# Two DMAs instead of eight for 128 rows of w4, and two instead of four for wo, in a decode kernel that is bound by its loads

## Chip, cores and metric

One core of one Trainium2 chip. The metric is the device time of one execution in microseconds (us). A kernel is run several times. The time given is the median of its runs. Smaller is better. "2%" is the size from which a change counts as faster or slower.

## The reference

One decode step for B = 4 sequences, D = 576, in bfloat16: sliding-window attention and an MLP side by side, summed. Cut to what matters:

```python
W = 2048                                  # window: the last 2048 of 8192 cached positions
q = (xn @ wq)                             # 32 heads of 128
k, v = k_cache[:, :, -W:], v_cache[:, :, -W:]      # 16 kv heads, 2 q heads share one
p = softmax(q @ k.T * 128 ** -0.5)
attn = (p @ v) @ wo                       # wo: 4096 x 576
mlp = gelu(layernorm(...) @ w3) @ w4      # w3: 576 x 4608, w4: 4608 x 576
out = x + attn + xn + mlp                 # the mixer between is zero for one position
```

All is done once per sequence, so each weight and each cached key and value is read once: 87.17 MB from HBM.

## The kernel before

It loads K and V one kv head at a time (2.1 MB, six buffers), in the order K0 K1 K2 V0 K3 V1 K4 ..., and the weights between them. All large loads are issued by SyncE (`nc.sync`) on one queue, and this queue serves the 16 DMA engines of the core. The last loads are six pieces of w4. Each output is the sum of many small matmuls that accumulate into `acc`.

`w4` has 4608 rows, 36 x 128. 35 blocks of 128 rows are loaded in pieces over all 16 engines. The last 128 rows, the "apart rows", are loaded by themselves, because which engines carry a DMA depends on its shape (in this trace such a DMA ends with 5, 3 or 1 semaphore packets instead of 16). With them the author fills up engines that would otherwise end early.

```python
# 100 rows over five engines ("A"), 12 over three ("C"), 16 on engine 0 alone (six pieces, "B")
def x4_rows(part):
    if part == "A":
        src = B_w4[X0 + 28:F, :].rearrange("(q g i) n -> g q (i n)", q=4, g=5)
        nc.sync.dma_start(out=t[0:NX, XA * D:XS * D], in_=src)
    elif part == "C":
        src = B_w4[X0 + 16:X0 + 28, :].rearrange("(q g) n -> g q n", q=4)
        nc.sync.dma_start(out=t[0:12, XC * D:XA * D], in_=src)
    else:
        q, lo, hi = part                  # two or four rows into one partition
        ...
X_AFTER = {13: ["A", (0, 0, 4)], 14: [(1, 0, 4), (2, 0, 2), "C"], 15: [(2, 2, 4), (3, 0, 2), (3, 2, 4)]}
...
wo_src = A_wo.rearrange("(s p i) n -> s p (i n)", p=P, i=WOR)    # four groups of 1024 rows
def load_wo(p):                                                  # before V0, V4, V8 and V12; two buffers
    t = wop.tile([P, WOR, D], BF16, tag="wo", name="wo_sb")
    nc.sync.dma_start(out=t[:].rearrange("p i n -> p (i n)"), in_=wo_src[p])
...
mlp_extra(XC, XS)         # 12 matmuls on the apart rows, ahead of the last V
...                       # last V, projection's preparation
mlp_extra(XB, XC)         # 8 matmuls of 4 rows
o_proj(hl)                # last projection with wo
for lo, hi in pieces:     # w4, 35 blocks x 2 matmuls
    mlp_out(lo, hi)
# then two casts of acc into fin, and the output DMA
```

By rows, the sixteen engines carry 40, 24, 24, 20, 20 apart rows on engines 0 to 4 and none on 5 to 15.

Of the kernel before, what the change touches and what calls it, by code (L numbers as in the profile page):

```python
# [11 lines left out]
BF16 = mybir.dt.bfloat16  # L12
# [10 lines left out]
def kernel(  # L23
# [14 lines left out]
    nc = tc.nc  # L38
    P = 128
    B, Sq, D = A_x.shape  # L40
# [4 lines left out]
    F = B_w3.shape[1]  # L45
# [30 lines left out]
    pad.tile([P, PAD], F32, name="pad")  # L76
    kvp = ctx.enter_context(tc.tile_pool(name="kv", bufs=NKV))
    wp = ctx.enter_context(tc.tile_pool(name="w", bufs=1))
    wop = ctx.enter_context(tc.tile_pool(name="wo", bufs=2))
    ktp = ctx.enter_context(tc.tile_pool(name="kt", bufs=2))  # L80
    ptp = ctx.enter_context(tc.tile_pool(name="pt", bufs=2))
    bigp = ctx.enter_context(tc.tile_pool(name="big", bufs=2))
# [8 lines left out]
    w_tiles = {}  # L91
    wo_tiles = {}
    kv_tiles = {}
    WOH = 8
    WOR = WOH
    WOD = P // WOH
    WOQ = WOH // rep
    wo_src = A_wo.rearrange("(s p i) n -> s p (i n)", p=P, i=WOR)

    def load_kv(kind, h):  # L100
        win = k_win if kind == "K" else v_win
        t = kvp.tile([P, NC, Dh], BF16, tag="kv", name=f"{kind.lower()}n")
        nc.sync.dma_start(out=t[:].rearrange("p c d -> p (c d)"),
                          in_=win[:, h].rearrange("b (p c) d -> p b (c d)", c=NC))
        kv_tiles[kind, h] = t

    first = wop.tile([P, WOR * D], BF16, tag="wo", name="first")
    cut = {"at": 0}

    def part(n, parts=P):  # L110
# [10 lines left out]
    nc.sync.dma_start(out=wq_sb[:, 0:KJ * NQ], in_=wq_main)  # L121

    def load_wo(p):
        t = wop.tile([P, WOR, D], BF16, tag="wo", name="wo_sb")
        nc.sync.dma_start(out=t[:].rearrange("p i n -> p (i n)"), in_=wo_src[p])
        wo_tiles[p] = t

    def load_w3():
        t = wp.tile([P, KJ * F + F // 2], BF16, tag="w", name="w3_sb")
        nc.sync.dma_start(out=t[:, 0:KJ * F], in_=B_w3[0:KJ * P, :].rearrange("(p j) f -> p (j f)", j=KJ))  # L130
        nc.sync.dma_start(out=t[:, KJ * F:], in_=B_w3[KJ * P:D, :].rearrange("r (e f) -> (r e) f", e=2))
        w_tiles["w3"] = t
# [1 line left out]
    NFM = NF - 1  # L134
    W4_PIECES = [0, NFH, NFM - 11, NFM - 6, NFM - 2, NFM - 1, NFM]
    X0 = F - P
    XB, XC, XA = 0, 4, 5
    XS = 10
    NX = 20
    NS = NFM + XS  # L140

    def x_cols(ap):
        b, c, a = ap[:, 0:16], ap[:, 16:28], ap[:, 28:P]
        return [(0, b.rearrange("p (q i) -> p i q", q=4)), (16, c.rearrange("p (q g) -> p g q", q=4)),
                (28, a.rearrange("p (q g i) -> p i g q", q=4, g=5))]

    def load_w4():
        t = wp.tile([P, NFM, D], BF16, tag="w", name="w4_sb")
        for lo, hi in zip(W4_PIECES, W4_PIECES[1:]):
            e = lo // NFH  # L150
            n = NFH - e
            src = B_w4[e * (F // 2):e * (F // 2) + P * n, :].rearrange("(p i) n -> p i n", i=n)
            nc.sync.dma_start(out=t[:, lo:hi, :], in_=src[:, lo - e * NFH:hi - e * NFH, :])
        w_tiles["w4"] = t

    def load_x4():
        t = kvp.tile([P, NC, Dh], BF16, tag="kv", name="x4")
        w_tiles["x4"] = t[:].rearrange("p c d -> p (c d)")

    def x4_rows(part):  # L160
        t = w_tiles["x4"]
        if part == "A":
            src = B_w4[X0 + 28:F, :].rearrange("(q g i) n -> g q (i n)", q=4, g=5)
            nc.sync.dma_start(out=t[0:NX, XA * D:XS * D], in_=src)
        elif part == "C":
            src = B_w4[X0 + 16:X0 + 28, :].rearrange("(q g) n -> g q n", q=4)
            nc.sync.dma_start(out=t[0:12, XC * D:XA * D], in_=src)
        else:
            q, lo, hi = part
            src = B_w4[X0 + 4 * q + lo:X0 + 4 * q + hi, :].rearrange("(q i) n -> q (i n)", q=1)  # L170
            nc.sync.dma_start(out=t[q:q + 1, (XB + lo) * D:(XB + hi) * D], in_=src)

    X_AFTER = {13: ["A", (0, 0, 4)], 14: [(1, 0, 4), (2, 0, 2), "C"], 15: [(2, 2, 4), (3, 0, 2), (3, 2, 4)]}


    ident_bf = const.tile([P, P], BF16)
# [22 lines left out]
    op = const.tile([P, WOR, B], BF16, name="op")  # L199
# [5 lines left out]
    def acc_of(i):  # L205
        return accs[i * 2 // NI][i * QD:i * QD + B, :]


    def acc_matmuls(terms):
        for lhsT, rhs in terms:  # L210
            for i in range(NI):
                nc.tensor.matmul(out=acc_of(i), lhsT=lhsT, rhs=rhs[:, i * CW:(i + 1) * CW],  # L212
                                 start=False, stop=False, skip_group_check=True)
# [44 lines left out]
    for kb in range(NQD):  # L258
        nc.gpsimd.tensor_copy(out=sel[:, :, :, kb, :],
                              in_=ident_bf[:].rearrange("p (ib i e) -> p ib e i", ib=2, e=2))  # L260
# [19 lines left out]
    with nc.allow_low_precision("zeros and ones"):  # L280
# [7 lines left out]
                          in_=sel_j[:].unsqueeze(1).to_broadcast([P, NG, NJ]))  # L288
# [38 lines left out]
    for r in range(2):  # L327
        nc.vector.tensor_copy(out=q_bf[:, r],
                              in_=qT_ps[:, r].rearrange("p u (g x) -> p g u x", g=NQD)[:, :, :, 0:B])
# [5 lines left out]
    for kb in range(NQD):  # L335
        rows = slice(kb * QD, (kb + 1) * QD)
        dst = qz[rows, ZP:].rearrange("p (x m) -> p x m", m=P)[:, :, kb * QD:kb * QD + NJ].rearrange("p x (b r) -> p x b r", r=rep)
        src = qs_ps[rows].rearrange("p h i r b -> p (h i) b r")
# [89 lines left out]
    def o_scale(h):  # L428
        O_sb[h] = bigp.tile([P, NSL, Dh], F32, tag="big", name="O_sb")
        nc.scalar.activation(out=O_sb[h][:], in_=O_ps.pop(h)[:], func=ACT.Copy, scale=st.pop(("rd", h)))  # L430
# [39 lines left out]
    def o_proj(h):  # L470
        if h % WOQ < WOQ - 1:
            return
        acc_matmuls([(op[:, i, :], wo_tiles[h // WOQ][:, i, :]) for i in range(WOR)])

    G_CHUNKS = [(e, 4 * g, 4) for e in range(2) for g in range(NQD)] + [(e, 16, 2) for e in range(2)]
    xs = const.tile([P, NS, B], F32, name="g_x")
# [33 lines left out]
    def mlp_turn(r):  # L510
        chunks = G_CHUNKS[r * NQD:(r + 1) * NQD]
        n, m = chunks[0][2], len(chunks)
        xn = XS if r == 2 else 0
        gT_all = ps_m.tile([P, n * m + xn, QD], F32, tag="m", name="gT_ps")
        gT_ps = gT_all[:, 0:n * m].rearrange("p (u g) x -> p u g x", u=n)
        gs = g_sb.pop(r)
        for u in range(n):
            nc.tensor.transpose(out=gT_ps[:, u].rearrange("p g x -> p (g x)"), in_=gs[0:m * QD, :, u],  # L518
                                identity=ident_f[0:m * QD, 0:m * QD])
        if r < 2:  # L520
            dst = xs[:, r * NFH:r * NFH + 16, :].rearrange("p (g u) b -> p u g b", u=n)
        else:
            e1 = slice(QD, 2 * QD)
            for s in range(XS):
                off, k = (4 * s, 4) if s < XC else (16, 12) if s == XC else (28 + NX * (s - XA), NX)
                nc.tensor.transpose(out=gT_all[0:k, n * m + s, :], in_=g_x[e1, off:off + k],
                                    identity=ident_f[e1, e1])
            for lo, hi, k in ((XB, XC, 4), (XC, XA, 12), (XA, XS, NX)):
                nc.scalar.activation(out=xs[0:k, NFM + lo:NFM + hi, :],
                                     in_=gT_all[0:k, n * m + lo:n * m + hi, 0:B], func=ACT.Copy)  # L530
            nc.scalar.activation(out=xs[:, NFM - 1, :], in_=gT_ps[:, 0, 1, 0:B], func=ACT.Copy)
            nc.scalar.activation(out=xs[:, 16:18, :], in_=gT_ps[:, :, 0, 0:B], func=ACT.Copy)  # L532
            return
        nc.vector.tensor_copy(out=dst, in_=gT_ps[:, :, :, 0:B])  # L534
# [7 lines left out]
        nc.gpsimd.tensor_scalar(out=u[:], in0=u[:], scalar1=0.5, scalar2=0.5, op0=ALU.mult, op1=ALU.add)  # L542
        nc.gpsimd.tensor_tensor(out=gT[:], in0=u[:], in1=xs[:], op=ALU.mult)

    def mlp_extra(lo, hi):
        t = w_tiles["x4"]
        acc_matmuls([(gT[0:k, NFM + s, :], t[0:k, s * D:(s + 1) * D])
                     for s in range(lo, hi) for k in (4 if s < XC else 12 if s == XC else NX,)])

    def mlp_out(lo, hi):  # L550
        w4 = w_tiles["w4"]
# [4 lines left out]
    for h in range(Hkv):  # L556
        order.append(("V", h))
        if h + 3 < Hkv:
            order.append(("K", h + 3))
        if h == min(X_AFTER):  # L560
            order.append(("X", h))
    W3_AFTER = ("V", 2)
    pos = {"n": 0, "free": NKV}

    def flush_loads():
        while pos["n"] < len(order) and pos["free"] > 0:
            kind, h = order[pos["n"]]
            if kind == "V" and h % WOQ == 0:
                load_wo(h // WOQ)
            if kind == "X":  # L570
                load_x4()
            else:
                load_kv(kind, h)
            if kind == "X" or kind == "V" and h > min(X_AFTER):
                for part in X_AFTER.get(h, []):
                    x4_rows(part)
            pos["n"] += 1
            pos["free"] -= 1
            if (kind, h) == W3_AFTER:
                load_w3()  # L580
        if pos["n"] == len(order):
            pos["n"] += 1
            load_w4()
# [4 lines left out]
    for t in range(Hkv):  # L588
        hm, hv, hf, hp = t - 1, t - 2, t - 3, t - 4
        for s in range(NSL):  # L590
# [40 lines left out]
            if t == G_AT:  # L631
                if s < 3:
                    mlp_g(s)
                if s > 0:
                    mlp_turn(s - 1)
                if s == NSL - 1:
                    mlp_act()
# [20 lines left out]
    sm_den(hl)  # L658
    sm_rec(hl)
    o_scale(hl - 1)  # L660
    mlp_extra(XC, XS)
    for s in range(NSL):
        pv(hl, s)
    o_scale(hl)
# [4 lines left out]
    o_sum(hl)  # L669
    o_spread(hl)  # L670
    o_pick(hl)
    mlp_extra(XB, XC)
    o_proj(hl)
    for lo, hi in pieces:
        mlp_out(lo, hi)
# [39 lines left out]
```

## Time and profile before

| | before |
|---|---|
| time, three runs | 211.31 us (211.28 to 212.18) |
| span of the profiled execution | 209.6 us |
| read from HBM | 87.17 MB |
| last data packet of a load ends | 206.30 us from the start |
| semaphore of the last load | 206.60 us |
| casts begin | 206.96 us |
| output DMA issued | 207.47 us |

The last four lines are the end of the kernel in order of time. Whatever is to make the kernel faster has to make the first of them earlier, or one of the steps between them shorter.

### The profile page before, as it was taken

What the parts mean: (1) busy time and instruction counts of PE and PEld (TensorE: products, weight loads), DVE (VectorE), ACT (ScalarE), POOL (GpSimd) and SP (SyncE); (2) the same over time, 40 slices, a digit from 0 to 9 for tenths busy, and PEclk for the clock granted to TensorE, in tenths of its full rate; (3) what the DMA queues carried; (4) which work ended last, traced back from release to release, by engine and by line L of the source; (5) the groups of instructions that cost most, each with busy time, mean ns of one, the idle gap of its engine ahead of it and who ended that gap; (6) DMA issues with size and microseconds to landing.
All of it is one profiled execution on the core that took longest, in us unless ns stands there. A gap on an engine that the chain in (4) does not pass through costs nothing.

```text
span 209.6 us, 2356 instructions
## 1 busy us (share of the span) xinstructions
PE 150.2 (72%) x958; PEld 58.2 (28%) x972; DVE 113.4 (54%) x156; ACT 34.8 (17%) x72; POOL 9.0 (4%) x32
## 2 busy tenths in 40 slices
PE   0357297699590039958998987589697955999693
PEld 0122132233140003213444332234232312343361
DVE  4511877894910083935608889176848390764200
ACT  7612201012010011110222221102111111023100
POOL 4710000000000000000002100000000000000000
PEclk9999589999787555788999999789978796699979
DMA  7999999999999999999999999999999999999992
GB/s 301 400 419 425 425 424 430 438 432 424 434 450 406 427 435 420 443 428 435 428 428 435 419 428 434 435 425 438 428 428 438 415 439 435 416 441 428 432 403 98
DMA packets 6702, 87.31 MB, mean 417 GB/s; under 512 B 758, under 2 KB 1034, under 8 KB 1700
## 3 DMA queue, kind: packets, MB, share of 16 engines
q1 hardware_dynamic: 6684, 87.17, 97.7%
q8 instruction: 7, 0.11, 0.2%
q10 hardware_dynamic: 8, 0.00, 0.0%
q14 instruction: 3, 0.02, 0.0%
HBM read 87.17 MB, written 0.00 MB: 416 GB/s over the span
## 4 chain that ended last, share of the span: by engine, by line
DMA 66%; DVE 15%; PE 14%; ACT 1%; issue 1%; SPq 1%; DVEq 0%; ACTq 0%
DMA kn<-in_A_k_cache_dram 43%; DVE kt L253 12%; DMA vn<-in_A_v_cache_dram 10%; DMA w_sb<-in_B_w_dram 7%; DMA wq_sb<-in_A_wq_dram 6%; PE S L366 5%; PE g_ps L496 2%; PE q_ps L310 2%; PE O L423 1%; PE oT L436 1%; DVE PT L400 1%; PE acc L212 1%; DVE mx L372 1%; PE S L388 1%; ACT E L395 1%
## 5 line engine op out<-in xcount | busy, mean ns | idle before, releaser
L366 PE MATMUL S<-kt,qz 128*128 128x512 bf16 x242 | 76.4, 437 | 32.2 <-DVE kt L253 30.4
L253 DVE STREAM_TRANSPOSE kt<-kn 128x2048 int32<-128x2048 int32 x32 | 73.4, 2297 | 24.3 <-DMA kn<-in_A_k_cache_dram 22.9
L366 PEld LDWEIGHTS <-qz 128*128 128x128 bf16 x256 | 23.5, 106 | 64.3 <-issue 47.7
L423 PE MATMUL O<-vn,PT 128*32 128x512 bf16 x256 | 23.9, 414 | 9.3 <-DMA vn<-in_A_v_cache_dram 9.3
L430 ACT ACTIVATE O_sb<-O,rd 128x512 f32<-128x512 f32 x16 | 11.0, 686 | 64.7 <-DVE rd L413 48.3
L395 ACT ACTIVATE E<-S 128x512 bf16<-128x512 f32 x16 | 9.5, 597 | 72.6 <-PE S L388 72.6
L400 DVE STREAM_TRANSPOSE PT<-E 128x512 bf16<-128x512 bf16 x16 | 11.4, 710 | 14.4 <-ACT E L395 14.4
L446 DVE TENSOR_REDUCE on<-oT 128x8 bf16<-128x128 f32 x16 | 4.6, 289 | 22.1 <-PE oT L436 21.9
L423 PEld LDWEIGHTS <-PT 128*32 128x32 bf16 x256 | 5.5, 95 | 33.0 <-issue 22.1
L436 PE MATMUL oT<-ident_w,O_sb 128*128 128x128 f32 x64 | 12.7, 331 | 0.3 <-ACT O_sb L430 0.3
L372 DVE TENSOR_REDUCE mx<-S 128x1 f32<-128x512 f32 x16 | 10.5, 659 | 1.1 <-PE S L366 1.1
L436 PEld LDWEIGHTS oT<-ident_w,O_sb 128*128 128x128 f32 x64 | 8.3, 165 | 5.2 <-issue 4.3
L388 PE MATMUL S<-nm,j_row 8*128 8x512 bf16 x16 | 6.7, 421 | 1.8 <-DVE nm L384 1.7
L354 PE MATMUL S<-negbig,ohT 4*128 4x512 bf16 x16 | 6.2, 384 | 0.0
L212 PE MATMUL acc<-w_sb,gT 128*4 128x288 bf16 x70 | 5.5, 311 | 0.6 <-DMA w_sb<-in_B_w_dram 0.6
L310 PE MATMUL q_ps<-wq_sb,xnT 128*32 128x512 bf16 x40 | 4.3, 611 | 2.2 <-DMA wq_sb<-in_A_wq_dram 2.2
L212 PE MATMUL acc<-wo_sb,op 128*4 128x288 bf16 x64 | 5.5, 324 | 0.4 <-DVE op L468 0.4
L496 PE MATMUL g_ps<-w_sb,ln2T 128*32 128x512 bf16 (+2 forms) x55 | 5.5, 441 | 0.0
L212 PEld LDWEIGHTS <-gT 128*4 128x4 bf16 (+3 forms) x90 | 4.2, 89 | 3.1 <-issue 1.0
L538 POOL TENSOR_TENSOR g_u<-g_x 128x180 f32<-128x180 f32 x1 | 0.5, 486 | 101.9 <-ACT g_x L532 101.9
L681 DVE CAST fin<-acc 4x288 bf16<-4x288 f32 x1 | 0.4, 446 | 8.1 <-PE acc L212 8.1
L534 DVE COPY g_x<-gT_ps 128x64 f32<-128x64 f32 x2 | 0.4, 223 | 7.5 <-PE gT_ps L518 7.5
(94 smaller groups left out, 79.3 us busy)
## 6 DMA issues: line engine op xcount, KB each, us to landing
kn<-in_A_k_cache_dram SPq DMA_DIRECT2D x16, 2048.0 KB, 25.9
vn<-in_A_v_cache_dram SPq DMA_DIRECT2D x16, 2048.0 KB, 22.7
wo_sb<-in_A_wo_dram SPq DMA_DIRECT2D x4, 1152.0 KB, 37.8
w_sb<-in_B_w_dram SPq DMA_DIRECT2D x1, 4608.0 KB
wq_sb<-in_A_wq_dram SPq DMA_DIRECT2D x1, 4096.0 KB
w_sb<-in_B_w_dram SPq DMA_DIRECT2D x1, 2592.0 KB, 11.0
w_sb<-in_B_w_dram SPq DMA_DIRECT2D x2, 576.0 KB, 34.3
w_sb<-in_B_w_dram SPq DMA_DIRECT2D x1, 864.0 KB
```

Source lines behind the costliest of these rows:

```text
L212: nc.tensor.matmul(out=acc_of(i), lhsT=lhsT, rhs=rhs[:, i * CW:(i + 1) * CW], start=False, stop=False, skip_group_check=True)
L253: nc.vector.transpose(out=kt[:], in_=src)
L310: nc.tensor.matmul(out=q_ps[r][g * QD:(g + 1) * QD, :], lhsT=xnT[:, k, :], rhs=wq_sb[:, col:col + NW], start=(j == 0), stop=False, skip_gr ...
L366: nc.tensor.matmul(out=S_ps[h][:], lhsT=qz[:, z0:z0 + P], rhs=kt[:, ib, c0:c0 + SC, e:2 * QD:2].rearrange("p c k -> p (c k)"), start=False ...
L372: nc.vector.reduce_max(out=mx[:], in_=S_ps[h][:], axis=AX.X)
L388: nc.tensor.matmul(out=S_ps[h][:], lhsT=j_row[:], rhs=st.pop(("nm", h))[:, 0:1].to_broadcast([NJ, NW]), start=False, stop=False, skip_grou ...
L395: nc.scalar.activation(out=E[h][:].rearrange("p c k -> p (c k)"), in_=S_ps.pop(h)[:], func=ACT.Exp, scale=scale, accum_out=st["rs"][:, h % ...
L400: nc.vector.transpose(out=PT[h][:], in_=E.pop(h)[:])
L423: nc.tensor.matmul(out=O_ps[h][g * QD:(g + 1) * QD], lhsT=PT[h][:, c, :], rhs=vn[:, :, c, :], start=(s == 0), stop=False, skip_group_check ...
L430: nc.scalar.activation(out=O_sb[h][:], in_=O_ps.pop(h)[:], func=ACT.Copy, scale=st.pop(("rd", h)))
L436: nc.tensor.transpose(out=oT[:, s, :], in_=o[:, s, :], identity=ident_w[:, s * NJ:s * NJ + P])
L496: nc.tensor.matmul(out=out, lhsT=ln2T[:, k, :], rhs=rhs, start=(j == 0), stop=False, skip_group_check=True)
```

## The change

Its intent is simplicity, without loss: eight loads of the apart rows become two, ten slots of matmuls become six, and wo needs half the DMAs. The 28 rows that had been on engines 0 (16) and 0 to 2 (12) are spread over seven engines, four rows each. Rows per engine become 24 on engines 0 to 4, and 4 on 5 and 6. All of them are issued at one place, after V13. wo comes as two tiles of 2.36 MB, before V2 and before V12, in one buffer instead of two. Cut to its core:

```diff
-    wop = ctx.enter_context(tc.tile_pool(name="wo", bufs=2))
+    wop = ctx.enter_context(tc.tile_pool(name="wo", bufs=1))
-    wo_src = A_wo.rearrange("(s p i) n -> s p (i n)", p=P, i=WOR)
+    wo_src = A_wo.rearrange("(t s p i) n -> t p s (i n)", s=2, p=P, i=WOR)
     def load_wo(p):
-        t = wop.tile([P, WOR, D], BF16, tag="wo", name="wo_sb")
+        t = wop.tile([P, 2, WOR, D], BF16, tag="wo", name="wo_sb")
 ...
-    XB, XC, XA = 0, 4, 5
-    XS = 10
+    XE, XS = 28, 6
 ...
-    def x4_rows(part):                    # with X_AFTER: eight DMAs after V13, V14 and V15
-        ...
+        for lo, hi, src in ((0, 1, B_w4[X0:X0 + XE, :].rearrange("(q g) n -> g q n", q=4)),
+                            (1, XS, B_w4[X0 + XE:F, :].rearrange("(q g i) n -> g q (i n)", q=4, g=5))):
+            nc.sync.dma_start(out=w_tiles["x4"][0:NX if lo else XE, lo * D:hi * D], in_=src)
 ...
+    WO_AT = [("V", 2), ("V", 12)]
-            if kind == "V" and h % WOQ == 0:
-                load_wo(h // WOQ)
+            if (kind, h) in WO_AT:
+                load_wo(WO_AT.index((kind, h)))
 ...
-    mlp_extra(XC, XS)
+    mlp_extra()
 ...
-    mlp_extra(XB, XC)
```

## The prediction

> **What bounds the kernel now.** I read the page's DMA rows first, because the kernel streams 87 MB of cache and weights through one core and every compute engine shows idle time.
>
> ```profile
> span 209.6 us, 2356 instructions
> PE 150.2 (72%) x958; PEld 58.2 (28%) x972; DVE 113.4 (54%) x156; ACT 34.8 (17%) x72; POOL 9.0 (4%) x32
> ...
> DMA  7999999999999999999999999999999999999992
> ...
> DMA packets 6702, 87.31 MB, mean 417 GB/s; under 512 B 758, under 2 KB 1034, under 8 KB 1700
> ...
> q1 hardware_dynamic: 6684, 87.17, 97.7%
> q8 instruction: 7, 0.11, 0.2%
> ```
>
> The 16 DMA engines are full from the first slice to the last but one. 97.7% of 16 engines' span leaves 0.023 x 209.6 = 4.8 us idle per engine, and that is the start (first data at 1.75 us) and the end (after 206.6 us), not a gap between. I cut the packet records into stretches of 2 us to be sure: from 4 us to 204 us the mean busy share never falls under 1.00. So the loads are never late in being issued; bytes, packets and the balance between the 16 engines set the time at which the last load lands.
>
> Then the order of time at the end, on the tensor engine:
>
> ```profile
> 193.02 0.90 PE L212 MATMUL acc<-x,gT 12*4 12x288 bf16 x12
> 194.65 1.05 PE L423 MATMUL O<-vn,PT 128*32 128x512 bf16 x16 [0.74 <-DMA vn<-in_A_v_cache_dram]
> ...
> 197.58 0.35 PE L455 MATMUL R<-on,sel_wo 128*128 128x32 bf16 x8 [0.38 <-DVE on L446]
> 197.86 0.65 PE L212 MATMUL acc<-x,gT 4*4 4x288 bf16 x8
> 198.90 2.08 PE L212 MATMUL acc<-wo_sb,op 128*4 128x288 bf16 x16 [0.39 <-DVE op L468]
> 200.78 4.53 PE L212 MATMUL acc<-w_sb,gT 128*4 128x288 bf16 x58
> 205.92 1.01 PE L212 MATMUL acc<-w_sb,gT 128*4 128x288 bf16 x12 [0.61 <-DMA w_sb<-in_B_w_dram]
> ```
>
> The last V lands at 194.6, PE works through to 205.3, waits 0.61 us for w4 and follows its last pieces. The semaphores of those pieces complete at 205.88, 206.24 and 206.60 us. After the last, two matmuls, the two casts, the output DMA and its landing take the 3.0 us to 209.6. The eight matmuls of 4 rows at 197.86 (the slots that disappear) lie in a time in which PE waits for DVE anyway: the output projection after them begins at 198.90, when DVE's `op` is ready.
>
> **What the Trainium skill says.** "DMA: Bandwidth & Descriptors", section "Why a DMA increments its semaphore by 16 and not by 1": a DMA runs on the largest k up to 16 that divides the outer dimensions, on the lowest-numbered k engines. So the old pieces run on engines 0-4, 0-2 and 0; the new ones on 0-4 (100 rows, 20 each) and 0-6 (28 rows, 4 each). The trace agrees as far as it can: a piece ends with 5, 3 or 1 four-byte packets, not 16. Section "Where 436 GB/s comes from" of the same page puts the ceiling of the 16 ports at 435 GB/s; here 16384-byte packets follow each other every 607 ns on an engine, 27.0 GB/s, 432 for 16. "Runtime: NRT & Kernel Launch", section "Instruction fetch mechanics": instructions come in 16 KiB blocks over the sequencer's own DMA queue. The trace shows seven packets of 16384 bytes on q8, and each throws one engine back (below).
>
> **The balance, which is all that the change can move.** In the packet records each engine follows a fixed beat, so its lag behind the others can be read from the times of the 16 four-byte packets that end each DMA. These lags stay the same to 2 ns over whole DMAs and jump only when something is put on one engine. Against the engine that ends first, the sixteen end at 0, 204, 338, 402, 1130, 1375, 1416, 1498, 1552, 1626, 1633, 1644, 1667, 1680, 1763 and 1850 ns. Going back through the jumps:
> - four (0 to 402) carry no apart rows and meet no instruction fetch;
> - seven (1375, 1416, 1552, 1626, 1633, 1667, 1850) met one fetch of q8 each, which cost 1.41 to 1.42 us in the last five cases (the first two blend with other jumps); the one at 1850 jumped by 1419 at 105 us and has no apart rows;
> - five (1130, 1498, 1644, 1680, 1763) jump by 0.87 to 1.80 us when the apart rows come: engines 0 to 4. Engine 0, with 40 rows, is the one at 1763. Three smaller fetches (8192 bytes) fall on engines 1 to 4 too, at 0.55 to 0.84 us each.
>
> So the old layout put the rows where no large fetch falls, and it fits well: engine 0 ends 87 ns before the last.
>
> **The change part by part.**
> 1. Rows of w4. A packet of 5760 bytes takes 216 ns on the beat, 4608: 174, 2304: 89, 1152: 47, a semaphore packet 6. Engine 0 before: 4 x 216 + 6 = 870 (100 rows), 4 x 47 + 6 = 194 (12 rows), 2 x 180 + 4 x 95 = 740 (16 rows), 1804 ns in all. After: 870 + 194 = 1064, so -740. Engines 1 and 2: 1064 before and after. Engines 3 and 4: 870 before, 1064 after, +194. Engines 5 and 6: 0 before, 194 after. The ends become 1763 - 740 = 1023 for engine 0; 1498 and 1644 (or which two of the five are engines 3 and 4: by the size of the jump, 870) 1692 and 1838. The maximum stays 1850 unless that engine is 5 or 6; then it is 2044. If the seven fetches go to neighbouring engines in turn, 5 to 11 or 9 to 15, engines 5 and 6 are the first two fetched (1626 and 1667, to 1820 and 1861) or have none. By that the end moves by 0 to +11 ns; at worst by +194.
> 2. wo in two DMAs. The same 512 packets of 9216 bytes, so no bytes and no packets of data saved: two semaphore packets fewer per engine, -12 ns. Order: groups 0 and 1 come before V2 instead of before V0 and V4, groups 2 and 3 before V12 instead of V8 and V12. V0 to K4 land 2.7 us earlier (8 x 347 ns), V2 to V3 2.7 us later, later ones as before; V8 to V11 2.7 us earlier. Steps need about 7 us of DVE against 9.7 us of loads (two of 4.86), so this is caught up. The second wo tile lands at about 169 us as the fourth does now, and its first user runs at 186.
> 3. One wo buffer instead of two. The first wo now overwrites the start's scratch space, whose last reader is done at 20.3 us; SP doesn't reach that DMA before K4 is issued at 27.00. The second waits for the projection of heads 4 to 7, as the fourth DMA does now at 145.2. No new wait.
> 4. Issuing. Eight fewer DMAs on SP. Eight semaphores are used in turn, and the first w4 piece waits for V14 to land (189.65) because it shares its semaphore; after, it shares with the second wo and can go out right after V15, near 180.5. The queue gets deeper by some 9 us, but it never ran dry, so this gives nothing.
> 5. PE: 8 matmuls of 280 ns (0.65 us with overlap) go at 197.86, in the shadow of DVE; 4 transposes and 2 copies go near 112 us, in a stage with 16 us and more of loads queued. Nothing on the path.
>
> Sum: -0.01 us for semaphores, 0 to +0.01 (at most +0.19) for the balance, 0 for the rest: 211.31 - 0.01 + 0.02 = 211.3 us.
>
> **Rivals.**
> - *The relief of engine 0 counts.* If engine 0 were the one that ends last, -740 ns would reach the end until the next engine takes over, at most 1850 - 1838 = 12 ns with engines 3 and 4 raised. So even then the time would stay 211.3. Against it: engine 0 is second.
> - *Engines 5 or 6 become the bound.* +0.19 us, 211.5. For: they get rows that they never had, and the trace doesn't number the engines. Against: the order of fetches argued above.
> - *A new wait starves the queue.* The 2.36 MB of wo between K4 and V2, or V2 to K5 landing 2.7 us later, could delay a buffer's release and so a load. It would have to eat the backlog: a K load lands 25.9 us after issue where 4.86 us are its own, so about 20 us are queued. I give 1 to 3 us of loss a chance of 3%.
> - *PE's end becomes the bound.* PE has 0.6 us in hand before w4; its clock was 0.73 of full between 200 and 204 us. If the throttle falls worse, the time grows by up to 1 us, in either kernel. That is run-to-run noise (before has one run at 212.18).
>
> **Range and chances.** The mechanisms move the time by at most 0.2 us, the repeats of before by 0.9. I take 210.9 to 211.9. 2% are 4.2 us; more than the whole idle time of the engines would have to come or go. Faster 0.01, within 2% 0.98, slower 0.01.
>
> **What would show each step right or wrong.** Still 97 to 98% on q1 and DMA at 9 in all inner slices; 6660 packets on q1 (6684, less 32 + 2 of semaphores, plus 48 - 38 for the apart rows); the spread of the 16 ends again near 1.85 us with engine 0 now in the middle near 1020; w4's first issue near 180 us; 12 matmuls on x near 193 and none at 198; the last w4 landing at 206.6 +- 0.2. A share in an inner slice under 9, SP waiting longer than now at the first wo or V2, or PE's idle time before w4 gone would prove it wrong.

## The result, and the profile after

| | before | after |
|---|---|---|
| time, six runs each | 211.28 us (211.14 to 212.18) | 211.62 us (211.46 to 211.68) |
| profiled execution: device time, span | 211.41, 209.6 | 211.59, 209.8 |
| last data packet of a load ends | 206.30 | 206.48 |
| casts begin | 206.96 | 207.15 |
| output DMA issued | 207.47 | 207.67 |

The ratio after to before is 1.0009, 95% interval 0.9992 to 1.0025: the same. Ratios here are the mean time of one kernel's fast runs over that of the other's of the same rounds, so they are not quite the ratio of the medians. The median of before lies 0.34 us lower here; in a later repeat (`after_again`) it was after that lay 0.02 us lower. What separates the two profiled executions, 0.18 us, is there at the last data packet already; the steps behind it are equal to a few hundredths.

The page of the kernel after, its rows on busy time, the clock, the DMA engines and the queues, to be held against the rows of before in the prediction:

```profile
span 209.8 us, 2335 instructions
...
PE 148.0 (71%) x960; PEld 56.6 (27%) x960; DVE 113.7 (54%) x156; ACT 34.8 (17%) x70; POOL 8.9 (4%) x32
...
DMA  7999999999999999999999999999999999999991
...
DMA packets 6678, 87.31 MB, mean 416 GB/s; under 512 B 724, under 2 KB 1016, under 8 KB 1676
...
q1 hardware_dynamic: 6660, 87.17, 97.5%
q8 instruction: 7, 0.11, 0.2%
```

There are 21 instructions fewer and 24 packets fewer, for the same bytes. PE is busy for 2.2 us less, but most of this is the clock that it was granted (0.886 on the mean instead of 0.868) and not the change: `x_only` below, with the same matmuls as the kernel after, was busy for 149.9 us at 0.866. The DMA row has hardly moved: the engines are as full as before, at the same rate. What was saved was saved where time costs nothing.

The order of time on PE at the end, after (start, length, instruction; in brackets the idle time before it and what ended that):

```profile
193.17 0.90 PE L199 MATMUL acc<-x,gT 28*4 28x288 bf16 x12
194.81 1.05 PE L410 MATMUL O<-vn,PT 128*32 128x512 bf16 x16 [0.74 <-DMA vn<-in_A_v_cache_dram]
...
199.07 1.15 PE L199 MATMUL acc<-wo_sb,op 128*4 128x288 bf16 x16 [0.97 <-DVE op L455]
200.86 3.10 PE L199 MATMUL acc<-w_sb,gT 128*4 128x288 bf16 x48 [0.65 <-DMA w_sb<-in_B_w_dram]
204.69 0.78 PE L199 MATMUL acc<-w_sb,gT 128*4 128x288 bf16 x10 [0.72 <-DMA w_sb<-in_B_w_dram]
206.09 1.03 PE L199 MATMUL acc<-w_sb,gT 128*4 128x288 bf16 x12 [0.62 <-DMA w_sb<-in_B_w_dram]
```

The eight matmuls at 197.86 are gone, and what grew is PE's idle time before the projection: 0.97 us of waiting for DVE's `op`, which comes when it came before (all of this stretch lies some 0.16 us later). PE then waits for w4 three times and ends with the last piece.

SyncE's issues in both kernels, from 160 us on (start, time that the group took with its waits, line, transfer; SPq is SyncE's sequencer). Before:

```profile
163.21 0.91 SPq L164 DMA_DIRECT2D x<-in_B_w_dram  x1
164.17 0.36 SPq L171 DMA_DIRECT2D x<-in_B_w_dram  x1
167.94 0.55 SPq L103 DMA_DIRECT2D vn<-in_A_v_cache_dram  x1
...
179.94 0.56 SPq L103 DMA_DIRECT2D vn<-in_A_v_cache_dram  x1
184.76 0.81 SPq L171 DMA_DIRECT2D x<-in_B_w_dram  x3
189.67 5.67 SPq L153 DMA_DIRECT2D w_sb<-in_B_w_dram  x6
```

After:

```profile
160.13 1.77 SPq L160 DMA_DIRECT2D x<-in_B_w_dram  x2
163.79 6.56 SPq L103 DMA_DIRECT2D vn<-in_A_v_cache_dram  x2
170.40 15.45 SPq L151 DMA_DIRECT2D w_sb<-in_B_w_dram  x6
```

The last V and the first piece of w4 are issued far earlier, the latter at 170.40 instead of 189.67, and w4 still lands 0.18 us later. This is what it looks like when a queue is never empty: an earlier issue only stands longer in the queue.

What decides the last landing is how long the slowest of 16 engines takes. I worked this out as in the prediction: from the records of packets, the lag of each engine behind the one that ends first, in ns, sorted. An "R" marks an engine with 20 or more apart rows:

```
before: 0 204 338 402 1130R 1375 1416 1498R 1552 1626 1633 1644R 1667 1680R 1763R 1850
after:  0 24 169 274 1051R 1076R 1211R 1500 1522 1585 1608 1629R 1635 1655 1662 2152R
```

In each case a lag is a sum of three terms: how far the engine lagged before the apart rows came, the rows' own time, and an instruction fetch if it met one later. Engine 0 before: -44 + 1804 gives its 1763 to within 3 ns. The last of after: 1086 + 1064 = 2152. So an engine with apart rows came last here, and its 1086 are a lag of about 0.25 us from the start of the kernel and an 8192-byte fetch of 0.83 us that it met at 49 us.

### The profile page after: what moved, and what is told of

The parts are those of the page before. It is cut to its first block, busy times and chain, and to the rows that moved or that the text cites. A ratio compares the mean times of both kernels' runs of the same rounds, so it can differ in the third digit from the quotient of the medians.

```text
span 209.8 us, 2335 instructions
## 1 busy us (share of the span) xinstructions
PE 148.0 (71%) x960; PEld 56.6 (27%) x960; DVE 113.7 (54%) x156; ACT 34.8 (17%) x70; POOL 8.9 (4%) x32
## 3 DMA queue, kind: packets, MB, share of 16 engines
q1 hardware_dynamic: 6660, 87.17, 97.5%
## 4 chain that ended last, share of the span: by engine, by line
DMA 60%; PE 20%; DVE 16%; ACT 2%; issue 1%; SPq 0%; ACTq 0%
DMA vn<-in_A_v_cache_dram 25%; DMA kn<-in_A_k_cache_dram 19%; DVE kt L240 12%; DMA w_sb<-in_B_w_dram 10%; PE S L353 8%; DMA wq_sb<-in_A_wq_dram 6%; PE g_ps L483 2%; PE O L410 2%; PE q_ps L297 2%; PE S L375 1%; DVE mx L359 1%; ACT E L382 1%; DVE PT L387 1%; PE acc L199 1%; PE oT L423 1%
## 5 line engine op out<-in xcount | busy, mean ns | idle before, releaser
L353 PE MATMUL S<-kt,qz 128*128 128x512 bf16 x256 | 77.5, 432 | 32.5 <-DVE kt L240 32.5
L410 PE MATMUL O<-vn,PT 128*32 128x512 bf16 x256 | 23.6, 411 | 10.2 <-DMA vn<-in_A_v_cache_dram 10.2
L423 PE MATMUL oT<-ident_w,O_sb 128*128 128x128 f32 x64 | 11.9, 314 | 0.3 <-ACT O_sb L417 0.3
L423 PEld LDWEIGHTS oT<-ident_w,O_sb 128*128 128x128 f32 x64 | 7.7, 157 | 4.8 <-issue 4.1
L199 PE MATMUL acc<-w_sb,gT 128*4 128x288 bf16 x70 | 4.9, 285 | 2.0 <-DMA w_sb<-in_B_w_dram 2.0
L199 PE MATMUL acc<-wo_sb,op 128*4 128x288 bf16 x64 | 4.6, 286 | 1.0 <-DVE op L455 1.0
L525 POOL TENSOR_TENSOR g_u<-g_x 128x164 f32<-128x164 f32 x1 | 0.5, 460 | 101.4 <-ACT g_x L519 101.4
L199 PEld LDWEIGHTS <-gT 128*4 128x4 bf16 (+2 forms) x82 | 3.6, 83 | 4.0 <-issue 2.8
```

What stands on the lines that cost most here:

```text
L199: nc.tensor.matmul(out=acc_of(i), lhsT=lhsT, rhs=rhs[:, i * CW:(i + 1) * CW], start=False, stop=False, skip_group_check=True)
L353: nc.tensor.matmul(out=S_ps[h][:], lhsT=qz[:, z0:z0 + P], rhs=kt[:, ib, c0:c0 + SC, e:2 * QD:2].rearrange("p c k -> p (c k)"), start=False ...
L410: nc.tensor.matmul(out=O_ps[h][g * QD:(g + 1) * QD], lhsT=PT[h][:, c, :], rhs=vn[:, :, c, :], start=(s == 0), stop=False, skip_group_check ...
L423: nc.tensor.transpose(out=oT[:, s, :], in_=o[:, s, :], identity=ident_w[:, s * NJ:s * NJ + P])
```

## The experiments

All twelve kernels give the right result. "Before" is the kernel before in the rounds of the same call.

| kernel | median (lowest to highest) us, runs | ratio to before, 95% interval | before |
|---|---|---|---|
| x_only | 212.18 (212.16 to 212.66), 6 | 1.0034, 1.0017 to 1.0051 | 211.55 |
| wo_only | 211.84 (211.42 to 212.59), 6 | 1.0015, 0.9995 to 1.0035 | 211.55 |
| after_again | 211.53 (211.29 to 211.67), 6 | 0.9996, 0.9980 to 1.0012 | 211.55 |
| pad2 | 212.08 (212.01 to 212.22), 6 | 1.0026, 1.0005 to 1.0047 | 211.40 |
| pad3 | 211.69 (211.53 to 212.27), 6 | 1.0010, 0.9990 to 1.0031 | 211.40 |
| x_only_pad1 | 211.80 (211.53 to 212.26), 6 | 1.0004, 0.9982 to 1.0025 | 211.60 |
| wo_only_again | 211.62 (211.17 to 212.01), 6 | 0.9994, 0.9974 to 1.0014 | 211.60 |
| even | 211.60 (211.56 to 212.18), 6 | 1.0007, 0.9989 to 1.0026 | 211.55 |
| bal | 211.81 (211.59 to 211.92), 5 | 1.0013, 0.9998 to 1.0028 | 211.46 |
| dose_e0 | 211.57 (211.45 to 212.46), 6 | 1.0008, 0.9985 to 1.0030 | 211.40 |
| dose_e04 | 213.28 (212.73 to 213.86), 6 | 1.0085, 1.0062 to 1.0108 | 211.40 |
| dose_e04_w3 | 213.55 (213.00 to 214.06), 6 | 1.0099, 1.0080 to 1.0117 | 211.46 |

My theory: the change is neutral, because the queue is always full and the balance stays as good as it was. A first rival: the two parts do move the time, and cancel each other. A second: the rows on engines 0 to 4, or those on 5 and 6, are what ends last.

### The parts alone

`x_only` has the new layout of the apart rows with the four wo loads of before. `wo_only` has the eight old DMAs with the two new wo loads. `after_again` is the kernel after, unaltered.

```diff
 # x_only, against the kernel after
-    wop = ctx.enter_context(tc.tile_pool(name="wo", bufs=1))
+    wop = ctx.enter_context(tc.tile_pool(name="wo", bufs=2))
-            if (kind, h) in WO_AT:
-                load_wo(WO_AT.index((kind, h)))
+            if kind == "V" and h % WOQ == 0:
+                load_wo(h // WOQ)            # and load_wo, wo_src, o_proj of before
 # wo_only, against the kernel after
-    XE, XS = 28, 6
+    XB, XC, XA = 0, 4, 5
+    XS = 10                                  # and x4_rows, X_AFTER, x_cols, mlp_extra of before
```

> New layout of the apart rows (5 and 7 DMA engines, six slots), wo as before (four DMAs, two buffers). Theory A (balance: the extra 194 ns on engines 3 and 4 plus their phase set the last landing): the +0.2 to +0.3 us of the whole change comes back here, time 211.4 to 211.7, and the last DMA engine to end is one that carries apart rows. Theory B (the new order of wo moves the start of the queue and with it the phases): no change against before within 0.1 us, about 211.3.

> Old layout of the apart rows (5, 3 and 1 engines), wo in two DMAs with one buffer. Theory A: as before, 211.2 to 211.4. Theory B: 211.5 to 211.7, as the whole change.

> The changed kernel once more, unaltered. If the 0.3 us of the medians is real it comes back at 211.5 to 211.7 against 211.1 to 211.3 in the same rounds, ratio 1.001 to 1.002; if it is scatter between builds or executions, the ratio lies at 1.000. The lags of the 16 engines show whether the phase of the engine that ended last (1.11 us behind before the apart rows) repeats from execution to execution.

`after_again` is the same as before. But each part alone came out slower, `x_only` by 0.34% with an interval that excludes zero; the 0.15% of `wo_only` are not clear of the noise. Neither of the two theories had foreseen 212.18 us. Two parts that are slower alone and neutral together need an explanation, and the two profiled executions were slow for different reasons.

**wo_only: the clock of the tensor engine.** The end of PE's order of time in `wo_only` (its profiled execution, 212.59 us, was the slowest of the six):

```profile
198.61 1.12 PE L212 MATMUL acc<-x,gT 4*4 4x288 bf16 x8
199.66 2.08 PE L212 MATMUL acc<-wo_sb,op 128*4 128x288 bf16 x16
201.54 6.44 PE L212 MATMUL acc<-w_sb,gT 128*4 128x288 bf16 x70
```

There is no wait for w4 in it: PE works through without a gap and the casts begin at 208.02 instead of 207.15 us in the kernel after, although the last packet came earlier, at 206.35 us. The view by windows shows why. Columns: window, its length, busy time of PE, PEld, DVE, ACT and POOL, with the number of instructions in brackets, granted clock of PE, DMA share, GB/s. `wo_only`:

```profile
195.40:198.80 3.40, 3.02 (x26) 1.92 (x20) 0.66 (x3) 0.69 (x1) 0.00 (x0) 0.50 0.95 405
198.80:202.20 3.40, 3.40 (x30) 1.66 (x28) 0.77 (x2) 0.00 (x0) 0.00 (x0) 0.50 0.96 398
202.20:205.60 3.40, 3.40 (x32) 1.85 (x28) 0.00 (x0) 0.00 (x0) 0.00 (x0) 0.50 0.91 367
```

The kernel after, in the same windows:

```profile
195.40:198.80 3.40, 2.06 (x28) 1.15 (x16) 1.21 (x4) 0.69 (x1) 0.00 (x0) 1.00 0.99 422
198.80:202.20 3.40, 2.48 (x38) 1.68 (x40) 0.21 (x1) 0.00 (x0) 0.00 (x0) 1.00 0.94 390
202.20:205.60 3.40, 2.55 (x40) 1.61 (x35) 0.00 (x0) 0.00 (x0) 0.00 (x0) 1.00 0.91 365
```

The clock was 0.50 for 10.2 us, three windows on end, and PE itself became the last to finish. The Trainium skill, "TensorE: Matmul & The Clock Gate", Part 1, section "What's actually happening", states a clock of either 4/8 or 8/8, set anew in windows of about 3.4 us from how busy the PE had been. The lengths agree: in the clock records of all 14 traces each full stretch at one clock is a multiple of 3.413 us. How they come about doesn't agree, of which more at the end of this document. The new wo loads alone don't bring such a stretch, nor are they needed for one: the kernel before had such a stretch too (198.7 to 202.2 us), `dose_e0`, a variant of the kernel after, had 10.2 us of it (194.1 to 204.3) and took 212.46 us where its median is 211.57, and `after`, `after_again`, `pad3` and `dose_e04`, all with the new wo loads, had none after 190 us. The clock explains the one profiled execution; the other five runs of `wo_only` (median 211.79) have no trace. Of the runs of before at 212.1 us and over (7 of its 50) none was profiled. Two of them (212.25 and 212.70) show a mean clock of 0.854, as do the profiled executions of `dose_e0` and of the repeat of `wo_only`, and are likely this state; four lie at 0.870 to 0.884, as ordinary runs do, and stay unexplained; for one no clock is on record.

**x_only: a standstill of SyncE.** Here PE's end is as in the kernel after, and four of six runs lie at 212.16 to 212.19, none under: this is not chance. The very end of `x_only` (order of time on all engines):

```profile
206.02 1.01 PE L199 MATMUL acc<-w_sb,gT 128*4 128x288 bf16 x12 [0.64 <-DMA w_sb<-in_B_w_dram]
...
207.06 0.45 DVE L664 CAST fin<-acc 4x288 bf16<-4x288 f32 x1 [7.06 <-PE acc L199]
...
208.00 0.31 SPq L667 DMA_DIRECT2D out_dram<-fin  x1
```

The same in the kernel after:

```profile
207.15 0.45 DVE L665 CAST fin<-acc 4x288 bf16<-4x288 f32 x1 [8.13 <-PE acc L199]
...
207.67 0.31 SPq L668 DMA_DIRECT2D out_dram<-fin  x1
```

From the cast's begin to the output DMA's issue are 0.94 us in `x_only`, and 0.52 in the kernel after. The semaphore of the cast comes at 207.54 in `x_only`, and then SyncE does nothing for 0.45 us. In the kernel after there is a gap of the same length *behind* the output DMA, from 208.06 to 208.52 between two semaphore instructions (they are in the trace's records; the view leaves them out). There it lies beside the flight of the output (landed at 208.96) and costs nothing. The guess: every so many instructions SyncE has to wait for its next block of instructions, and the number of DMAs issued decides where this falls. The next runs test it.

### Moving the standstill

If the guess is right, DMAs that are added and do next to nothing must move the standstill: a few of them in the kernel after must bring it ahead of the output DMA and cost about 0.45 us, one more must hide it again, and one added to `x_only` must make `x_only` good. If the standstill is an effect of the transfers or of wo, none of this happens. `pad2` and `pad3` add two and three DMAs of 16 rows of 64 bytes to the kernel after. `x_only_pad1` adds one to `x_only`.

```diff
 # at the end of load_x4; N = 2 and 3
+        for c in range(N):
+            nc.sync.dma_start(out=w_tiles["x4"][16 * c:16 * c + 16, XS * D:XS * D + 32],
+                              in_=B_w4[16 * c:16 * c + 16, 0:32])
 # x_only_pad1: the same with N = 1, in x_only
```

> The changed kernel with two more tiny DMAs (64 bytes to each of 16 rows) after the apart rows; they change no result. Theory C (SyncE's instruction block): in x_only SyncE stood still for 0.45 us between the end of its last wait and the output DMA, in the changed kernel the same standstill lies two instructions later, behind the output DMA. Two more DMAs shift it to just ahead of the output DMA: the output DMA is issued 0.4 to 0.5 us after the cast ends, time 0.4 to 0.5 us above the changed kernel, 212.0 to 212.1. Rival (the 0.6 us of x_only came from the order of wo or from balance): no change, 211.5 to 211.7, and the output DMA is issued within 0.1 us of the cast's end.

> The same with three tiny DMAs. Theory C: the standstill moves ahead of SyncE's long wait for the end and is hidden again; the time is that of the changed kernel within 0.1 us, 211.5 to 211.7, below pad2 although it issues one DMA more. Rival (each DMA more costs): above pad2. It is also the control of the two doses below, which have three more DMAs as well.

> x_only with one tiny DMA more (64 bytes to each of 16 rows, read by nobody). Theory C: the standstill of SyncE, which in x_only lies just ahead of the output DMA, moves ahead of its long wait and is hidden: the output DMA is issued within 0.1 us of the cast's end, and the time falls by 0.4 to 0.5 us from 212.18 to 211.6 to 211.8 although there is one DMA more. Rival (the layout alone, without the new order of wo, costs 0.6 us): 212.1 to 212.3 again.

The last lines of the three, `pad2`:

```profile
206.94 0.45 DVE L667 CAST fin<-acc 4x288 bf16<-4x288 f32 x1 [7.30 <-PE acc L201]
...
207.88 0.30 SPq L670 DMA_DIRECT2D out_dram<-fin  x1
```

`pad3`:

```profile
207.02 0.45 DVE L667 CAST fin<-acc 4x288 bf16<-4x288 f32 x1 [8.12 <-PE acc L201]
...
207.56 0.29 SPq L670 DMA_DIRECT2D out_dram<-fin  x1
```

`x_only_pad1`:

```profile
207.23 0.45 DVE L665 CAST fin<-acc 4x288 bf16<-4x288 f32 x1 [7.07 <-PE acc L200]
...
207.77 0.30 SPq L668 DMA_DIRECT2D out_dram<-fin  x1
```

Cast to output: 0.94, 0.54 and 0.54 us. With two more DMAs the kernel after is at 212.08, with three it is back at 211.69: a kernel with *more* to do is 0.39 us faster. `x_only` falls from 212.18 to 211.80 with one DMA more, and its ratio to before from 1.0034 to 1.0004. So the number of instructions on SyncE sets where the standstill falls, and it accounts for some 0.4 of the 0.6 us that `x_only` was over before. `even` below, with one DMA fewer than the kernel after, fits too: there the gap lies one semaphore instruction further back, from 208.08 to 208.53. That it is the fetch of an instruction block is argued from its shifting with the count; no record of the trace names it.

To see whether the wo loads cost anything once the clock is left out, `wo_only` was run again without an edit:

> wo_only once more, unaltered: its first six runs lay between 211.42 and 212.59, and in the profiled one the tensor engine ran 195.4 to 205.6 us at half clock and finished 1.3 us after the last landing without waiting for w4. If that is what makes the high values, a profile with the clock at full in that stretch comes with about 211.4 to 211.8 and PE waiting for w4 at the end; if wo's order itself costs 0.3 us, the median is again 211.7 or more with PE waiting.

It came out at 211.62 beside 211.60 of before. Its profiled execution, 212.01 us, was the slowest of its six and once more one with 10.2 us of half clock (193.8 to 204.1), so a profile of `wo_only` at full clock is not on record. By the interval of the repeat the wo loads cost at most 0.3 us; no cost is to be seen. Of the first rival little is left: with the standstill out of the way `x_only` is worth nothing that can be seen, and neither is `wo_only` in its repeat. Why the other runs of its first session lay higher is not shown.

### The balance of the engines

`even` spreads the 128 apart rows over all 16 engines, in one DMA and one slot. It takes away what the layouts are tuned for. By the numbers of before, engines that meet a large fetch should then get rows on top of it and come last.

```diff
-    XE, XS = 28, 6
+    XE, XS = P, 1
-        for lo, hi, src in (...):
-            nc.sync.dma_start(out=w_tiles["x4"][0:NX if lo else XE, lo * D:hi * D], in_=src)
+        nc.sync.dma_start(out=w_tiles["x4"][:, 0:D], in_=B_w4[X0:F, :])
```

> The changed kernel with the 128 rows spread over all 16 engines, 8 rows each (one DMA, one slot of 128 rows). Balance theory: each engine pays 8 x 47 + 6 = 382 ns, so the engines that met an instruction fetch and had no rows (1662 ns behind the first at the end) become the last at about 2.04 us, engine 3 or 4 falls from 2152 to about 1.47 us; the last landing moves by about -0.1 us, time 211.5. Rival (even loads are best because all engines are alike): 0.3 us or more below the changed kernel.

211.60, the same as before, and the last packet at 206.41: within 0.11 us of before and 0.07 of after. The engine that ended last was indeed one that had met a 16384-byte fetch (at 123 us), but 1.78 us behind the first, not 2.04 as expected: with rows on all engines the first one ends later too.

`bal` goes the other way. It tunes the layout anew: rows 40, 28, 28, 16, 16 on engines 0 to 4, with the new wo loads. Engines 3 and 4 get fewer, since one of them had ended last in `wo_only` (1289 + 870 ns; 870 are 20 rows), and engine 0 gets back what it had before.

```diff
-    # the three parts of the kernel before
+    XG = [(12, 4, 1, 3), (36, 12, 3, 3), (80, 20, 5, 4)]     # rows, partitions, engines, rows per partition
+    # one loop over XG in load_x4, six DMAs, ten slots as in the kernel before
```

> The changed kernel with the apart rows laid out by what the traces showed: 12 rows on engine 0, 36 on 0 to 2, 80 on 0 to 4, so 40, 28, 28, 16 and 16 rows on engines 0 to 4 (six DMAs, ten slots). Balance theory: engine 3 or 4, last at 2.15 behind the first with 24 rows, loses 8 rows (0.35 us) and ends near 1.8, engine 1 or 2 near 1.8 too, the others at 1.66: the last landing moves from about 206.5 to about 206.2 us, time 211.2 to 211.4. SyncE's standstill lies ahead of its long wait (four DMAs more than the changed kernel) and is hidden. Rival (the end is set elsewhere): 211.5 to 211.7 as the changed kernel, or 212.2 where the tensor engine runs its end at half clock.

It gained nothing: 211.81 beside 211.46. In its profiled execution engine 0, which carries the 40 rows, ended last: it had lagged by 590 ns since 33 us from the start, its rows took 1788, and its last data packet ended at 206.52. (The 590 count from the engine that was first until the rows came; from the one that ended first it was 2178 in all.) In before engine 0 had come to its rows first of all, 44 ns ahead of the engine that ended first. Such lags differ between executions of one program too: in `after` the engine that met the fetch at 49 us had lagged by 279 ns before it, in `after_again` by 438. So does who meets the large (16384-byte) fetches: engines 5 and 6 had both met one in `after_again`, one of them in `after`, none in `x_only`, with the same layout of rows. What did hold in the executions that were taken apart (those of before, `after`, `after_again`, `x_only`, `wo_only` and its repeat, `bal` and `dose_e0`) is that the 16384-byte fetches fell on engines without a large share of rows, and the 8192-byte ones on engines 0 to 4. Where the rows tell these apart (before, `wo_only`, its repeat and `bal`), the fetch at 48 to 50 us fell on engine 3 or 4 each time. In all of these but before an engine with many rows ended last, at 1.8 to 2.2 us behind the first, be its rows 20 (`wo_only`) or 40 (`bal`).

Then doses, to measure what a load on certain engines costs at the end. `dose_e0` adds three packets of 5760 bytes to engine 0 of the kernel after, and `dose_e04` adds three to each of engines 0 to 4. Both add three DMAs to SyncE, so that `pad3` and not `after` is their control.

```diff
 # r = 1 (dose_e0) or 5 (dose_e04), at the end of load_x4
+        for c in range(3):
+            dose = B_w4[128 * c:128 * c + 5 * r, :].rearrange("(g i) n -> g (i n)", i=5)
+            nc.sync.dma_start(out=w_tiles["x4"][r * c:r * c + r, XS * D:(XS + 5) * D], in_=dose)
 # dose_e04_w3: the same size from another weight
+            dose = B_w3[5 * c:5 * c + 5, 0:5 * D]
```

> The changed kernel with three DMAs of one packet of 5760 bytes each that run on engine 0 alone (data that nobody reads): 3 x (216 + 6) = 666 ns on engine 0. Balance theory: engine 0 ends some 1.0 to 1.1 us behind the first, the last at 2.15 to 2.2, so nothing happens: the last landing and the time as in pad3 within 0.1 us. Rival (total bytes or the busiest low engine sets the end): up to +0.67 us.

> The same doses on engines 0 to 4 (five packets a DMA): 666 ns on each. Balance theory: the engine that ends last in the changed kernel is one of these five, so the last landing moves by +0.6 to +0.7 us and so does the time, 212.1 to 212.4. Rival (the last engine is one without apart rows, as in before): it has 0.5 us in hand, and the time grows by 0.1 to 0.2 us only.

`dose_e0`: 211.57 against 211.69 of `pad3`, nothing. Engine 0 ended at 1776 ns with 1730 of rows and dose; another was last, at 2018. So engine 0 had room for these 0.67 us in this execution, and the prediction's -740 ns on it was rightly worth nothing.

`dose_e04`: 213.28, 1.59 us over `pad3`, and the last packet at 207.89 instead of 206.35. The end does hang on these engines. But three packets and three semaphores are 3 x 216 + 3 x 6 = 666 ns, and it cost more than twice that. In the records of packets some 40 packets, of all engines and not only of the dosed ones, took 50 to 450 ns over their usual time between 184.2 and 185.9 us; this moved the first-ending engine too, to 204.94 us (204.30 in `pad3`). One explanation was the source: the dose reads rows of w4 that the pieces read again. `dose_e04_w3` takes them from w3 instead.

> dose_e04 again, but the 15 packets are read from rows of w3 9216 bytes apart, not from three runs of 25 rows of w4. In dose_e04 some 40 packets of all engines ran 50 to 450 ns over their usual time just while the doses were read. If the source was the cause, those slow packets are gone and the time is 212.3 to 212.5 (pad3 plus 0.67); if any dose on five engines slows all, they stay and the time is about 213.2 again.

It is as slow, 213.55, with as many slow packets at the same time (46 that took 20 ns or more over their usual time; 45 in `dose_e04`). The source is not the cause. What slows these packets stays open, and so does the size of this cost; that a load on engines 0 to 4 reaches the end, and one on engine 0 alone doesn't, is shown.

No version beat both kernels.

## Why the prediction was right

It named 211.3 us; the kernel after took 211.62 and 211.53, and both lie in the range of 210.9 to 211.9. The number alone says little: what the change moved in the profile (0.18 us) is less than the runs of one kernel differ among themselves, so it would have come out right with a somewhat wrong mechanism too.

- **The bound.** Right. 97.5% of the engines' span on the queue and 9 in all inner slices, as before. Issuing w4 19 us earlier and taking eight matmuls from PE's end moved the last landing by no more than the balance of the engines accounts for.
- **Rows of w4.** The sizes were right: the row engines of the kernel after carry 1064 ns each, engines 5 and 6 carry 194 (one went from 1414 to 1608). An engine with rows and no late fetch ended at 1051 and another at 1076, near the 1023 told for engine 0. What was wrong is "the maximum stays 1850". It was 2152, of an engine with 1064 ns of rows, because the prediction took each engine's lag without rows from one execution as fixed: 772 was the largest of these on a row engine before, 1086 after, 1140 in the repeat. The term that was mis-sized is the lag that an engine brings along beside its fetch, from the start and from what the first-ending engine lost itself: for the row engine that met the fetch at 48 to 50 us it was -0.07 us before and 0.25 after, while the fetch took 0.84 and 0.83. The end moved by +0.18 us in the profile, not by 0 to +0.01, and just under the +0.19 that was called the worst, for another reason.
- **Engines 5 and 6.** "The first two fetched or none" was wrong: one of them was fetched in `after`, both in the repeat, none in `x_only`. They were last in none.
- **wo in two DMAs, one buffer.** Right as far as the runs resolve it: `wo_only_again` 211.62 against 211.60, and the DMA row of the kernel after stays at 9.
- **Issuing.** The first w4 piece was told for 180.5 us and came at 170.40; the last V too was issued some 10 us earlier than assumed. Worth nothing, as told.
- **PE.** Right: 12 matmuls at 193.17, none at 198, their time in the wait for DVE.
- **Counts and landing.** Right: 6660 packets, last landing 206.78 in 206.6 +- 0.2. The spread of the ends was 2.15 and not 1.85 us.
- **The rivals.** Engine 0's relief counts for nothing (`dose_e0`). "PE's end becomes the bound" does happen, in single executions with 10.2 us of half clock, and costs 0.4 to 0.9 us, told as up to 1 us. Not foreseen: the standstill of SyncE. By luck it falls behind the output DMA in this kernel; two more DMAs made it a loss of 0.4 us (`pad2`).

## What to carry to other kernels

Where one queue of loads kept all DMA engines full to the end, as here, fewer DMAs, fewer matmuls and earlier issues were worth nothing that could be measured, and could be taken for simplicity alone. A balance between engines that is tuned on one trace to tenths of a microsecond fits that one execution: look at several before tuning, as the lags from the start change from one to the next, and with some engines whether they meet an instruction fetch. And if a small edit changes the time by 0.4 us for no visible reason, look whether the last DMA of the program is issued late, and add or remove an instruction on its engine before looking for a deeper cause.

## What the Trainium skill lacked or had wrong

- "Runtime: NRT & Kernel Launch", section "Instruction fetch mechanics", calls the crossing of a 16 KiB boundary "mostly hidden". On the DMA engines it isn't: in a kernel bound by them each 16384-byte fetch that can be read singly set one engine back by 1.41 to 1.42 us, and each 8192-byte one by 0.55 to 0.84 us. And a standstill of 0.45 us on SyncE, which shifts with its number of instructions and may be the same crossing, was exposed ahead of the output DMA in `x_only` (212.18 us) and `pad2` (212.08), and hidden in `pad3` (211.69).
- No page says on which DMA engines these fetches fall, or that this changes from one execution to the next: with one layout of rows, engines 5 and 6 met two large fetches, one, or none.
- "TensorE: Matmul & The Clock Gate", Part 1, has the clock go up after one busy window of about 3.4 us. In `wo_only` PE was busy for 3.40 of 3.40 us by the profile, at clock 0.50, and the window after it was at 0.50 again; in the kernel after windows of 2.06 to 2.55 us were followed by full clock. In this kernel the busy time that the profile shows doesn't foretell the clock. (The profile models the ends of matmuls, so its busy time needn't be what the clock goes by.)
- No page has what slowed some 45 packets on all engines for about 2 us in `dose_e04` and `dose_e04_w3`, at a cost of 1.6 us where 0.67 were loaded.
